# Transformer layers on one core: w2 loaded in blocks of six, and the task scheduler's cost model and priorities replaced

## The chip, the cores and the metric

The kernel runs on one core of a Trainium2 chip. The metric is the device time of one execution in microseconds (us), as the median of several executions. The changed kernel is timed in the same way. A difference counts as faster or slower when it exceeds 2%.

The engines are named as in the profile: PE is the matrix engine, PEld its weight loads, DVE the vector engine, ACT the activation engine, POOL the general-purpose engine, SP the engine that here does nothing but issue transfers (DMA).

## The reference

Two kinds of layer alternate on 2048 tokens of width 576, and the pair is run twice with the same weights. The core of it:

```python
def _A_ref(x, wqkv, wo):            # H = 32 heads of Dh = 18, window W = 256
    qkv = (x @ wqkv).reshape(B, S, 3, H, Dh) ...
    scores = jnp.einsum("bhqd,bhkd->bhqk", q, k) * (Dh ** -0.5)
    mask = (idx[:, None] - idx[None, :] >= 0) & (idx[:, None] - idx[None, :] < W)
    p = _softmax(jnp.where(mask, scores, -1e9), axis=-1)
    o = jnp.einsum("bhqk,bhkd->bhqd", p, v)
    return o.reshape(B, S, D) @ wo

def _B_ref(x, w1, b1, w2, b2):      # D = 576, F = 4608
    y = _layernorm(x)
    h = _gelu(jnp.einsum("bsd,df->bsf", y, w1) + b1)
    return jnp.einsum("bsf,fd->bsd", h, w2) + b2

x = x + _A_ref(_layernorm(x), A_wqkv, A_wo)
x = x + _B_ref(_layernorm(x), B_w1, B_b1, B_w2, B_b2)
x = x + _A_ref(...); x = x + _B_ref(...)      # the same once more
```

So there is sliding-window attention with many small heads, and a large MLP whose second norm is applied to a layer-normed input.

## The kernel before

The 16 token tiles of 128 rows are cut into chunks of four tiles. Two layer pairs make eight chunks, numbered 0 to 7. Each chunk passes through these parts, and the parts of neighbouring chunks overlap:

- **q**: the projections to q, k and v, five matmuls of 288 columns for each half (line 665), copied out of PSUM by DVE (lines 687, 700); q and k are then transposed by transfers issued on SP (line 707).
- **ea, eb**: attention for head groups 0 to 3 and 4 to 7. Scores are four row-tiled matmuls at a time (line 735), exp on ACT (744), window masks on POOL (765), then the products with v (782), all into the PSUM bank 7. DVE divides by the row sums (792, 797) into `attq`.
- **t**: the tail. `attq` is transposed to `attT` by a transfer on SP (826), multiplied by wo (665), added to the residual (816), normalised (603, 608) and transposed again (623).
- **ga, gb**: the first MLP matmul for each half of F (lines 863 and 875), gelu on ACT (878).
- **ma, mb**: the second MLP matmul with w2 for each half (903), added to the residual (816, or 819 for the last layer).

Nothing of this order is written down by hand. Every piece is a task with an engine, the names it reads and writes, an estimated cost and a priority. A list scheduler in Python runs when the kernel is built, keeps a clock for each engine, takes the task that can start first (ties by priority), and so fixes the order of instructions on each engine and which PSUM bank each accumulation uses. The chip executes these fixed orders, with semaphores for the dependencies. The estimated costs are used for nothing else.

```python
key = (round(st, 3), t.prio, t.idx)
...
if t.eng == "pe" and st < self.warm_until and st - free["pe"] > 0.4:
    self.keep_warm(free["pe"], st, bank_free, extra)     # adds idle-filling matmuls (line 567)
```

Until a modelled time of 140 us the scheduler fills gaps that it expects on PE with matmuls on a tile of zeros (`warm`). Their results are not used.

The part that handles a transfer in the model, and the load of w2, are the places where the change acts:

```python
            if t.dma is not None:
                if t.eng == "sp":
                    over = sum(q[2] for q in queued) + t.desc - self.ring
                    # ... cut: waits until the ring has room ...
                done = max(dma_free, st + t.cost + t.lat) + t.move
                ...
                dma_free = done if t.eng == "sp" else dma_free + t.move
```

```python
    def w2_load(hf, prio, gate=False):
        for pr in range(NFH // 2):                          # NFH = 18
            f0 = hf * NFH + 2 * pr
            dma("sp", w2_sb[:, 2 * pr:2 * pr + 2, :], B_w2[f0 * P:(f0 + 2) * P, :].rearrange("(w p) d -> p w d", p=P),
                reads=[f"h{2 * pr}"] if gate else [], writes=[f"w2s{pr}"], cls="w2", ring=9, cost=0.55, lat=2.0, move=0.88, desc=256, prio=prio)
```

The second MLP matmul reads w2 in groups of six of these row tiles:

```python
                for f0 in range(0, NFH, 6):
                    def fn(e, hh=hh, b=b, f0=f0, i=i):
                        for fl in range(f0, f0 + 6):
                            ins = e.matmul(bank(b)[:, 0:HB], hT[:, fl, i * 128:(i + 1) * 128], w2_sb[:, fl, hh * HB:(hh + 1) * HB],
                                           start=(fl == 0), stop=(fl == NFH - 1))
                    add("pe", fn, reads=[f"h{fl}" for fl in range(f0, f0 + 6)] + [f"w2s{fl // 2}" for fl in range(f0, f0 + 6)], writes=[b],
                        cost=6 * mm_cost(HB), prio=prio + 0.05 * i, alloc=((b,) if f0 == 0 else ()))
```

`PL.nudge` is a table of numbers added to the priorities of named parts of named chunks ("t0", "q4.3", "ma3"), found by a search over the model.

The softmax here doesn't subtract the row's maximum and nothing guards it: scores larger than these inputs give would overflow.

## Time and profile before

| what | value |
|---|---|
| time, median of 3 | 945.84 us (945.45 to 946.3) |
| span of the profiled execution | 940.9 us |
| PE busy | 910.2 us, 97% of the span, 9394 matmuls |
| ACT busy | 593.4 us, 63% |
| POOL busy | 372.1 us, 40% |
| DVE busy | 319.3 us, 34% |
| mean granted clock of PE | 0.996 |
| moved by DMA | 130.10 MB, mean 138 GB/s |

The profile page gives busy time for each engine, then the span in 40 slices, the DMA queues, the chain of work that ended last, the costliest groups of instructions, and the transfers. [...] 2304 matmuls of mean 287 ns are busy for only 318.0 us. How closely matmuls follow one another is read from the distance between their starts. The list of waits says for how long an engine stood idle and what ended that.

### The profile page before, as it was taken

The page shows a single profiled execution, that of the slowest core. Times are in us where ns is not written, and L with a number is a line of the kernel's source. Part 1 is how long each engine was busy: PE and PEld are TensorE (multiplying, and loading weights), DVE is VectorE, ACT ScalarE, POOL GpSimd, SP SyncE. Part 2 cuts the span into 40 slices and gives each one's busy share as a digit, 9 for nine tenths or more (in the row PEclk, how much of TensorE's full clock was granted, in tenths as well). Part 3 has the DMA queues.
Part 4 walks back from the last instruction along what each step waited for, and adds up shares of the span by engine and source line. Part 5 has one row for each costly group of instructions (what it writes and reads, how often), then busy time and mean ns, then how long its engine had stood idle before and what let it go on. Part 6 is the DMA issues. An engine that isn't in the chain of part 4 may idle for free. (4 is left out here: it accounts for less than half of the span.)

```text
span 940.9 us, 22724 instructions
## 1 busy us (share of the span) xinstructions
PE 910.2 (97%) x9394; PEld 559.5 (59%) x9394; DVE 319.3 (34%) x796; ACT 593.4 (63%) x717; POOL 372.1 (40%) x507
## 2 busy tenths in 40 slices
PE   9888998999999999989999999999999999999998
PEld 6555474664755747455674666656566574656556
DVE  6647132641217511154420832135132330241001
ACT  3787675576756658656465567756776587852541
POOL 3877352353514425144250644515443163720100
PEclk9999999999999999999999999999999999999999
DMA  9995729725196160965439434594526916094440
GB/s 225 153 219 113 212 60 247 191 56 169 21 218 163 16 204 13 249 130 140 133 45 270 79 93 123 99 252 77 158 71 121 252 52 203 13 233 140 151 140 26
DMA packets 232470, 130.10 MB, mean 138 GB/s; under 512 B 142384, under 2 KB 230192, under 8 KB 232368
## 3 DMA queue, kind: packets, MB, share of 16 engines
q1 hardware_dynamic: 223056, 120.96, 53.8%
q0 software_dynamic: 6880, 5.03, 3.7%
q10 hardware_dynamic: 2432, 2.65, 0.9%
q8 instruction: 75, 1.23, 0.5%
q14 instruction: 27, 0.22, 0.1%
HBM read 91.87 MB, written 2.36 MB: 100 GB/s over the span
## 5 line engine op out<-in xcount | busy, mean ns | idle before, releaser
L744 ACT ACTIVATE pT<-ps 128x1024 bf16<-128x1024 f32 (+2 forms) x384 | 348.3, 970 | 138.7 <-PE ps L735 137.6
L765 POOL TENSOR_SCALAR_AFFINE_SELECT pT<-pT 128x512 bf16<-128x512 bf16 (+1 forms) x368 | 281.8, 789 | 288.9 <-ACT pT L744 258.8
L903 PE MATMUL ps<-w_sb,hT 128*128 128x288 bf16 x2304 | 318.0, 287 | 3.1 <-DVE x_res L816 1.8
L878 ACT ACTIVATE hT<-ps,b1col 128x512 bf16<-128x512 f32 x288 | 197.0, 688 | 176.1 <-PE ps L875 175.9
L875 PE MATMUL ps<-xnTm,w_sb 128*128 128x512 bf16 x1152 | 263.8, 380 | 0.0
L903 PEld LDWEIGHTS ps<-w_sb,hT 128*128 128x128 bf16 x2304 | 212.0, 98 | 74.8 <-issue 15.1
L875 PEld LDWEIGHTS ps<-xnTm,w_sb 128*128 128x128 bf16 x1152 | 106.2, 98 | 142.0 <-issue 26.6
L816 DVE TENSOR_TENSOR x_res<-ps,x_res 128x288 f32<-128x288 f32 x160 | 71.2, 449 | 312.0 <-PE ps L903 242.9
L665 PE MATMUL ps<-wqkv,xnTa 128*128 128x288 bf16 x960 | 136.9, 288 | 6.3 <-DVE qn L700 4.1
L665 PEld LDWEIGHTS ps<-wqkv,xnTa 128*128 128x128 bf16 x960 | 86.4, 98 | 42.5 <-DVE qn L700 8.6
L782 PEld LDWEIGHTS ps<-vA,pT 128*128 128x128 bf16 x2880 | 94.8, 96 | 25.3 <-issue 9.7
L782 PE MATMUL ps<-vA,pT 128*128 128x20 bf16 x2880 | 100.4, 171 | 3.5 <-POOL pT L765 2.7
L700 DVE CAST qn<-ps 128x288 bf16<-128x288 f32 x120 | 54.3, 455 | 106.1 <-PE ps L665 103.5
L885 POOL TENSOR_TENSOR x_res<-x_res,b2bc 128x576 f32<-128x576 f32 x32 | 44.9, 1402 | 97.1 <-ACT hT L878 97.1
L735 PE MATMUL ps<-qT,kT 32*128 32x384 bf16 (+2 forms) x1216 | 64.4, 277 | 3.4 <-DMA kT<-qn 1.2
L591 POOL TENSOR_SCALAR vtmp<-mv_all 128x1 f32<-128x1 f32 (+1 forms) x43 | 8.8, 205 | 116.9 <-DVE mv_all L582 115.7
L665 PE MATMUL ps<-wo_sb,attT 128*128 128x288 bf16 x320 | 45.5, 289 | 6.7 <-DMA attT<-attq 5.8
L580 DVE BATCH_NORM_STATS2 st_all<-x_res 128x6 f32<-128x288 f32 x104 | 44.8, 447 | 7.5 <-DMA x_res<-in_A_x_dram 6.3
L863 PE MATMUL ps<-xnTm,w_sb 64*128 64x512 bf16 x288 | 45.3, 384 | 1.0 <-ACT pT L744 0.7
L603 DVE TENSOR_SCALAR xn<-x_res,mv_all,rstd 128x576 bf16<-128x576 f32 x52 | 38.9, 754 | 15.2 <-DMA xnTm<-xn 5.8
L665 PEld LDWEIGHTS ps<-wo_sb,attT 128*128 128x128 bf16 x320 | 29.6, 98 | 19.9 <-DMA attT<-attq 6.7
L819 DVE TENSOR_TENSOR xn<-ps,x_res 128x288 bf16<-128x288 f32 x32 | 14.4, 454 | 77.2 <-PE ps L903 75.6
(39 smaller groups left out, 270.3 us busy)
## 6 DMA issues: line engine op xcount, KB each, us to landing
w_sb<-in_B_w_dram SPq DMA_DIRECT2D x144, 288.0 KB, 4.5
w_sb<-in_B_w_dram SPq DMA_DIRECT2D x72, 512.0 KB, 4.5
w_sb<-in_B_w_dram SPq DMA_DIRECT2D x144, 32.0 KB, 4.1
x_res<-in_A_x_dram POOLq DMA_DIRECT2D x4, 1152.0 KB, 7.8
out_dram<-xn SPq DMA_DIRECT2D x16, 144.0 KB, 1.8
wqkv<-in_A_wqkv_dram ACTq DMA_DIRECT2D x3, 576.0 KB, 7.2
hT<-in_A_x_dram SPq DMA_DIRECT2D x2, 576.0 KB, 4.4
wo_sb<-in_A_wo_dram ACTq DMA_DIRECT2D x1, 576.0 KB, 6.6
```

What stands on the lines that cost most here:

```text
L665: ins = e.matmul(bank(bs[o])[:, 0:HB], lhs(c), rhs(c, o * HB), start=(c == 0), stop=(c == KD - 1))
L700: add("dve", lambda e, b=bs[o], dst=dst: e.tensor_copy(dst, bank(b)[:, 0:HB].rearrange("p (h d) -> p h d", d=DH)), reads=[bs[o]], writes=[ ...
L735: ins = e.matmul(two(bs[j // 2])[:, j % 2, col:col + nq * 128], k_of(T0 + so)[0][32 * j:32 * j + 32, g, :], qs[32 * j:32 * j + 32, g, qo * ...
L744: add("act", lambda e, h2=h2: e.activation(pT[:, sl, 2 * h2:2 * h2 + 2, lo:hi], two(bs[h2])[:, :, lo:hi], ACT.Exp, scale=SCALE), reads=[bs ...
L765: add("pool", lambda e, ap=ap, pat=pat, sgn=sgn, kind=kind: e.affine_select(ap, ap, pattern=pat, compare_op=(ALU.is_ge if kind == "d" else ...
L782: ins = e.matmul(bank(B_O)[:, o:o + VW], pT[:, sl, j, col + qi * 128:col + (qi + 1) * 128], vA[:, (T0 + so) % VS, 4 * g + j, :], start=(fi ...
L816: add("dve", lambda e: e.tensor_tensor(x_res[:, t, sl], bank(b)[:, 0:HB], x_res[:, t, sl], ALU.add), reads=[b], writes=[f"x{t}h{hh}"], cos ...
L863: ins = e.matmul(bank(bk)[:, 0:n], w1_sb[64 * b:64 * b + 64, sl, col:col + 128], xnTm[64 * b:64 * b + 64, k % 2, 4, 0:n], start=True, stop ...
L875: ins = e.matmul(bank(bk)[:, 0:n], w1_sb[:, sl, col:col + 128], xnTm[:, k % 2, c, 0:n], start=False, stop=(c == 3))
L878: add("act", lambda e, ff=ff, fl=fl, bk=bk: e.activation(hT[:, fl, 0:n], bank(bk)[:, 0:n], ACT.Gelu_apprx_tanh, bias=b1col[:, ff:ff + 1]), ...
L885: add("pool", lambda e, t=t: e.tensor_tensor(x_res[:, t, :], x_res[:, t, :], b2bc[:, :], ALU.add), reads=["b2", f"h{fs[0]}"], writes=X(t), ...
L903: ins = e.matmul(bank(b)[:, 0:HB], hT[:, fl, i * 128:(i + 1) * 128], w2_sb[:, fl, hh * HB:(hh + 1) * HB], start=(fl == 0), stop=(fl == NFH ...
```

## The change

The change has two parts. It computes the same thing.

**w2 in blocks of six.** Each half of w2 (18 row tiles of 128 x 576) is loaded by three transfers of six tiles instead of nine of two, so that one transfer brings just what one group of six matmuls reads.

**The scheduler's model and priorities.** The costs of the tasks are replaced by values taken from traces aligned with the tasks one by one. A latency between an engine's end and the next engine's start is given separately (`lat`). The model of the transfers keeps one queue for each issuing engine, lets queues that are busy at once slow each other down, and limits the ring for each. The table of priorities was searched anew, under random delays of the transfers. None of these numbers exists on the chip. They act only through the order of tasks, the choice of PSUM banks and the number of idle-filling matmuls.

```diff
-        for pr in range(NFH // 2):
-            f0 = hf * NFH + 2 * pr
-            dma("sp", w2_sb[:, 2 * pr:2 * pr + 2, :], ..., reads=[f"h{2 * pr}"] if gate else [], writes=[f"w2s{pr}"],
-                cls="w2", ring=9, cost=0.55, lat=2.0, move=0.88, desc=256, prio=prio)
+        for b in range(NFH // WB):                          # WB = 6
+            f0 = hf * NFH + WB * b
+            dma("sp", w2_sb[:, WB * b:WB * b + WB, :], ..., reads=[f"h{WB * b}"] if gate else [], writes=[f"w2s{b}"],
+                cls="w2", ring=NFH // WB, cost=0.55, lat=2.0, move=0.44 * WB, desc=128 * WB, prio=prio)
...
-reads=[...] + [f"w2s{fl // 2}" for fl in range(f0, f0 + 6)]
+reads=[...] + [f"w2s{f0 // WB}"]
...
-                done = max(dma_free, st + t.cost + t.lat) + t.move
-                if t.eng == "sp":
-                    queued.append((done - t.move, done, t.desc))
-                dma_free = done if t.eng == "sp" else dma_free + t.move
+                at = max(served.get(t.eng, 0.0), st + t.cost + min(t.lat, 2.0))
+                done = at + t.move
+                for o in served:
+                    if o != t.eng and served[o] > at:
+                        both = min(t.move, served[o] - at)
+                        served[o] += both
+                        done += both
+                served[t.eng] = done
+                q.append((done - t.move, done, t.desc))
+                done += max(0.0, t.lat - 2.0)
... (costs; some of them)
-  bn_stats cost=0.43            +  cost=0.37, lat=0.14
-  xd (64 columns) cost=0.12     +  cost=0.38, lat=0.14
-  copies of q, k, v cost=0.42   +  cost=0.375, lat=0.14
-  exp cost=0.12 + 2*n*0.00083   +  cost=0.07 + 2*n*0.00083, lat=0.17
-  gelu cost=0.2 + n*0.00087     +  cost=0.145 + n*0.00087, lat=0.17
-  residual cost=0.46            +  cost=0.375, lat=0.14
... (priorities; the first of some 50 each)
-    PL.nudge = {"ld0+": 36.49, "eb0": 11.82, "q1.0": -3.43, ..., "t0": -24.79, "ea1": -30.85, ...}
+    PL.nudge = {"le0+": 14.98, "q1.0": -6.62, "q1.1": 0.41, ..., "t0": 4.51, "ga0": -13.62, ...}
```

(The `...` inside a line, and the lines that start with it, mark cuts; the costs are condensed.)

## The prediction

> **What bounds the kernel now.** I read the page's busy shares first, then the matmul groups by shape, then the list of PE's waits, then the timeline around the two longest waits. The page's first part and slices (columns: busy us, share, instructions; then tenths per slice):

> ```profile
> PE 910.2 (97%) x9394; PEld 559.5 (59%) x9394; DVE 319.3 (34%) x796; ACT 593.4 (63%) x717; POOL 372.1 (40%) x507
> PE   9888998999999999989999999999999999999998
> PEclk9999999999999999999999999999999999999999
> ```

> PE is the bound from end to end, at full clock. No other engine passes 63%, so only two things can shorten this kernel: fewer or closer-packed matmuls, and fewer PE waits. The chain that ended last says the same (PE 19% of the span, everything else about 0%, though it reaches back only to 755 us).

> "97% busy" hides slack, since matmuls overlap. I took the start-to-start distance of every pair of neighbouring matmuls in the trace: 122 ns for 288 columns behind 288, 216 ns for 512, 25 ns for the 20-column products, about 220 ns for a 288-column one ahead of a row-tiled score (about 95 ns of changeover). Taking for each pair of kinds the lower quartile of these distances (the mean inside row-tiled packs), the old order adds up to 893.1 us. PE's matmuls run from 1.1 us to 937.6 us, that is 936.5 us. So 936.5 - 893.1 = **43.4 us are lost** to waits and slow stretches, and 3.3 us follow the last matmul (one addition, one output transfer). The largest visible losses (columns: us in total, times, longest us):

> ```profile
> PE ps L665 <- DMA attT<-attq: 5.8, 2, 3.1
> PE ps L665 <- DVE qn L700: 4.1, 9, 0.9
> PE ps L782 <- POOL pT L765: 2.7, 8, 0.6
> PE ps L735 <- DMA kT<-qn: 2.1, 2, 1.2
> PE ps L903 <- DVE x_res L816: 1.8, 4, 1.1
> PE ps L735 <- ACT pT L744: 1.6, 6, 0.4
> PE ps L903 <- DVE xn L819: 1.3, 1, 1.3
> ```

> The idle gaps of PE add up to 27.4 us, 11.4 of them in the first 100 us. There is one large item, the attT transposes: twice PE came to the wo product too early. The SP queue and PE around the second (start us, us, engine, line, operation):

> ```profile
> 402.22 1.68 SPq L707 DMA_TRANSPOSE kT<-qn  x1
> 404.00 1.73 SPq L524 DMA_DIRECT2D w_sb<-in_B_w_dram  x3
> 405.84 6.01 SPq L826 DMA_TRANSPOSE attT<-attq  x4
> ...
> 410.11 0.79 PE L665 MATMUL ps<-wo_sb,attT 128*128 128x288 bf16 x5 [2.68 <-DMA attT<-attq]
> ```

> `attq` was ready at 402.33 us, but a k transpose and three weight loads stood ahead in SP's fixed order; the transpose issued 3.5 us later and PE ran dry at 407.4.

> [...] The trace has 4.5 us for 288 KB, and 4.5 for 512 KB[...].

> **The change part by part.**

> *w2 blocks.* 144 issues become 48. At a median 0.515 us each (the weight issues in SP's queue) SP saves 96 x 0.515 = 49 us of issuing. SP only issues, and PE never waited visibly for w2, so it is worth nothing directly. The bytes are unchanged. The matmuls already read in sixes, so a slot comes free no later than before. [...] I compared the order of both programs, counting PE work (by the distances above) between the matmul that releases a w2 slot and the first matmul that reads the new content. The shortest was 7.8 us and is 7.1 us, in chunk 0's ma, where the load waits for the gelu; every other is over 10 us. There a wait of some 0.8 us is possible.

> *Same matmuls, other order.* The instruction counts of PE, ACT, DVE and POOL are equal, but for the zeros: 62 become 50. The old trace has them at 107 to 205 ns. Summing the new order with the same distances gives 890.3 us. **Gain 893.1 - 890.3 = 2.8 us** (2.6 of it zero matmuls; the changeovers to scores are equal within 0.2).

> *attT.* PE work between a chunk's last product with v and the first wo product, chunks 0 to 7, was 3.5, 6.6, 22.5, 4.8, 15.2, 6.2, 14.5, 6.7 us and is 6.9, 21.1, 7.0, 10.4, 12.6, 25.6, 10.8, 7.6. The two waits above belong to chunks 1 and 3 (6.6 and 4.8). A free queue needs about 5.1 us: 1.0 us for the division (in chunk 1 the last product with v ends at 152.09 us, the division at 153.09) and 4.0 us median to landing; in chunk 0, whose 3.5 us other waits stretched to 5.1 (68.6 to 73.69 us), PE did not wait for attT. The new minimum is 6.9. Directly ahead of the new chunk 3 transpose stands a q transpose instead of loads. I count **5.6 of the 5.8 us as gained**.

> *PSUM banks that DVE must empty.* DVE needs about 0.7 us. Old places with no PE work at all between use and reuse by the projections: 3 (two in chunk 7, 0.55 us idle each); new: 1, in the first chunk. **Gain 1.4 us**, with refill.

> *q and k transposes.* Old shortest distances 2.6 and 3.8 us, both waited (0.9 and 1.2). New: 4.9 and 5.0. **Gain 1.0 us**, but one of the new ones is at the start of chunk 7 (q at 5.6 and 6.1): **loss 0.8**.

> *The 1.3 us wait on L819* (DVE held by an xn slot still being transposed): half gained, 0.7.

> *New short distances.* Behind gb of chunk 0 a w2 group follows its gelu's matmul by 0.33 us (gelu takes 0.69) and a score reuses a bank written just before: 1.0 us. The bank of the v products is reused after 0.6 to 1.0 us four times where the division needs 1.0: 0.8 us. w2 above: 0.8 us. **Loss 2.6 us.**

> Sum: -2.8 - 5.6 - 1.4 - 1.0 - 0.7 + 0.8 + 2.6 = -8.1 us, all on PE and so on the path. 945.84 - 8.1 = **937.7 us**.

> **The rivals.**

> *A: the losses only move.* A new order has new near-misses, and distances do not show queueing behind ACT or the transfers. For it: 20 of the 27.4 us idle were many waits under 1.3 us that no one planned. Against: the new costs lie closer to the trace (the 64-column norm takes 0.468 us; the model had 0.12 and now 0.38 + 0.14). Then the gain is the 2.8 us alone: 943.

> *B: the blocks delay transposes.* 864 KB ahead of k, q or att transposes makes them late, and PE waits more for DMA. In the new order a block stands between the attT transposes of chunks 3, 4 and 5. For it: both old attT waits came from loads ahead. Against: the work to hide them is 10 us and more there. Two waits of 3 us: about 944; four: 950.

> *C: the better model removes most avoidable waits.* Of the 43.4 us lost, some 11 us in the first 100 us come from dependencies with little else to do, and about 12 us are not at task starts at all. That leaves about 20 us. Removing two thirds of it and the 2.8 us: 930.

> **Range and chances.** 937.7 lies between A and C. B and C are tails. I take 931 to 946. For over 2% the time must fall under 926.9, 18.9 us less, nearly all of the avoidable part: 0.05. Over 964.8 needs a systematic new wait, which the distances do not show: 0.02. The rest, 0.93, is within 2%.

> **What would show it.** In the changed profile: PE's wait for attT near 0 (step attT); 50 zero matmuls and the group about 2 us less busy; w2 transfers x48 at 864 KB landing in 5 to 7 us, without a PE wait for them over 1 us; idle gaps of PE near 20 us; start-to-start of 122 and 216 ns unchanged. Wrong would be: PE waits on DMA over 6 us (B), or idle about 27 us with other names (A), or under 14 us (C). Another granted clock would make it wrong for a reason outside all of this.

## The result, and the profile after

The changed kernel takes **938.13 us** (937.28 to 941.76) against 945.68 us for the kernel before, timed beside it: a ratio of 0.9926, with a 95% interval of 0.990 to 0.9953. Two further jobs with the unchanged pair gave 941.54 against 946.38 us (0.9947, 0.993 to 0.9965) and 940.42 against 944.68 us (0.9948, 0.993 to 0.9965). So the gain is 0.5 to 0.7%, which is 7.6, 4.8 and 4.3 us between the medians and "same" at the 2% line. The prediction was 937.7 us, a gain of 8.1 us.

The first part and two slice rows of the page after (busy us, share, instructions; then tenths per slice), and its first transfer:

```profile
PE 903.7 (96%) x9340; PEld 560.0 (60%) x9382; DVE 317.6 (34%) x796; ACT 593.8 (63%) x717; POOL 372.8 (40%) x507
...
PE   8888999999998999999999999999999999999998
...
PEclk9999999999999999999999999999999999999999
...
w_sb<-in_B_w_dram SPq DMA_DIRECT2D x48, 864.0 KB, 6.2
```

The program has 9382 matmuls, as PEld shows. 42 matmul records are missing from this profile, so the lower busy time of PE is no gain. The span of this execution is 939.8 us against 940.9 before, only 1.1 us less. It was the slowest of its four executions, and the profiled one of before (942.8 us) was faster than all its timed ones. A third profile of the changed kernel has all its records and a span of 936.5 us. The twelve largest of PE's waits in that one (us, times, longest us; xnTa and xnTm are the transposed normalised inputs of attention and of the MLP, w_sb holds the weights of the MLP, pT the exp of the scores):

```profile
PE ps L745 <- ACT pT L754: 3.5, 12, 0.5
PE ps L675 <- DVE qn L710: 3.2, 7, 0.9
PE ps L913 <- DMA w_sb<-in_B_w_dram: 2.3, 2, 1.3
PE ps L675 <- DMA xnTa<-xn: 2.1, 1, 2.1
PE ps L675 <- DVE x_res L826: 1.7, 2, 1.1
PE ps L873 <- DMA xnTm<-xn: 1.4, 1, 1.4
PE ps L745 <- issue: 1.2, 1, 1.2
PE ps L792 <- DVE attq L807: 1.1, 2, 0.8
PE ps L576 <- DVE warm L571: 1.1, 1, 1.1
PE ps L745 <- DMA kT<-qn: 1.0, 1, 1.0
PE ps L745 <- DVE xn L829: 1.0, 1, 1.0
PE ps L675 <- DMA attT<-attq: 0.9, 1, 0.9
```

The wait for attT fell from 5.8 us to 0.9 here (2.7 and 1.2 in the two other profiles). But 2.1, 1.4 and 2.3 us for xnTa, xnTm and w_sb stand where before there were 0.4 us for xnTa and none for the others. PE's idle gaps add up to 27.3 us in this profile and 27.4 in the first one of before. **The waits changed their names, and their sum did not fall.** (The other profiles of both kernels lack 42 records each, which lengthens the gaps: 31.2 us before, 32.7 and 32.5 us after.) That made the near-hit suspicious, and the experiments ask where the time really came from.

### The profile page after: what moved, and what is told of

The parts are those of the page before. It is cut to its first block, busy times and chain, and to the rows that moved or that the text cites. A ratio compares the mean times of both kernels' runs of the same rounds, so it can differ in the third digit from the quotient of the medians.

```text
span 939.8 us, 22499 instructions
## 1 busy us (share of the span) xinstructions
PE 903.7 (96%) x9340; PEld 560.0 (60%) x9382; DVE 317.6 (34%) x796; ACT 593.8 (63%) x717; POOL 372.8 (40%) x507
## 5 line engine op out<-in xcount | busy, mean ns | idle before, releaser
L912 PE MATMUL ps<-w_sb,hT 128*128 128x288 bf16 x2304 | 314.8, 286 | 2.0 <-DMA w_sb<-in_B_w_dram 1.0
L884 PE MATMUL ps<-xnTm,w_sb 128*128 128x512 bf16 x1110 | 259.3, 381 | 3.8 <-issue 1.9
L674 PE MATMUL ps<-wqkv,xnTa 128*128 128x288 bf16 x960 | 134.8, 288 | 7.4 <-DVE qn L709 3.6
L744 PE MATMUL ps<-qT,kT 32*128 32x384 bf16 (+2 forms) x1216 | 64.2, 277 | 6.0 <-ACT pT L753 2.1
L801 DVE RECIPROCAL rinv<-ps 128x16 f32<-128x16 f32 x64 | 16.3, 255 | 115.3 <-PE ps L791 114.8
L696 DVE CAST vA<-ps 128x288 bf16<-128x288 f32 x64 | 28.9, 455 | 76.3 <-PE ps L674 76.2
L611 DVE TENSOR_SCALAR xn<-x_res,mv_all,rstd 128x576 bf16<-128x576 f32 x52 | 36.1, 694 | 21.1 <-DMA xnTm<-xn 16.1
```

Of the source, the lines that this page charges most:

```text
L674: ins = e.matmul(bank(bs[o])[:, 0:HB], lhs(c), rhs(c, o * HB), start=(c == 0), stop=(c == KD - 1))
L744: ins = e.matmul(two(bs[j // 2])[:, j % 2, col:col + nq * 128], k_of(T0 + so)[0][32 * j:32 * j + 32, g, :], qs[32 * j:32 * j + 32, g, qo * ...
L884: ins = e.matmul(bank(bk)[:, 0:n], w1_sb[:, sl, col:col + 128], xnTm[:, k % 2, c, 0:n], start=False, stop=(c == 3))
```

## The experiments

Each was timed in five rounds beside the kernel before; a job is a set of versions timed together on one chip. Line numbers differ between runs, since each edit shifts the lines. "Clock" is the mean granted clock of PE over all timed executions. "Lost" is (1 - clock) x 940 us, the full-speed time that the throttle took away. The kernel before had 946.38 us and clock 0.9947 in job 1, 947.32 and 0.9942 in job 2, 944.68 and 0.9952 in job 3.

| run (job) | us | ratio | 95% interval | clock | lost, us |
|---|---|---|---|---|---|
| before again (1) | 946.82 | 1.0008 | 0.9992 to 1.0024 | 0.9945 | 5.2 |
| changed again (1) | 941.54 | 0.9947 | 0.9930 to 0.9965 | 0.9968 | 3.0 |
| old order, w2 in sixes (1) | 948.49 | 1.0018 | 1.0003 to 1.0033 | 0.9940 | 5.6 |
| new order, w2 in pairs (1) | 939.84 | 0.9933 | 0.9905 to 0.9960 | 0.9973 | 2.5 |
| before without mid zeros (2) | 949.88 | 1.0026 | 1.0009 to 1.0043 | 0.9924 | 7.1 |
| changed without mid zeros (2) | 936.67 | 0.9903 | 0.9879 to 0.9928 | 0.9968 | 3.0 |
| before, attT first (2) | 943.25 | 0.9966 | 0.9951 to 0.9981 | 0.9969 | 2.9 |
| new model, old priorities (2) | 958.47 | 1.0138 | 1.0103 to 1.0173 | 0.9933 | 6.3 |
| before, waits filled with zeros (3) | 940.96 | 0.9958 | 0.9942 to 0.9973 | 0.9989 | 1.0 |
| changed, third time (3) | 940.42 | 0.9948 | 0.9930 to 0.9965 | 0.9966 | 3.2 |
| pairs, no mid zeros (3) | 937.52 | 0.9911 | 0.9889 to 0.9933 | 0.9972 | 2.6 |
| the same, last attT first (3) | 937.51 | 0.9917 | 0.9897 to 0.9937 | 0.9970 | 2.8 |

### Both kernels again

No edit. Expected of the changed kernel and of the kernel before:

> The changed kernel itself, timed in five rounds, with a second profile. Its first profile has a span of 939.8 us, 4 us above two of its other executions, with a new wait of 2.7 us for an attT transpose and the clock down in two slices. Theory 1 (the gain is the new order of instructions): 0.992 of the time before, and a profile whose PE waits for attT, xnTa and xnTm are smaller than in the first profile when its span is nearer to 936 us. Rival (the gain is luck of the executions): 0.996 or more.

> The kernel before itself, with a second profile. Its first profile was an execution of 942.8 us, 3 us below its median. All theories: a ratio of 1.000 within the interval, which shows the noise. Theory 1: the waits of PE that vary between its two profiles are those for transfers (attT, kT, xnTa), by some 3 us in sum, and the waits for DVE and ACT repeat within 1 us.

The gain held at 0.53%, less than theory 1 expected but clear of the rival, and the kernel before repeated itself at 1.0008. In the changed kernel's second profile the wait for attT is smaller than in the first, as theory 1 had it (1.2 us), but the one for xnTa is larger (2.7 us, 2.1 in the first). Before's second profile has an attT wait of 5.9 us, so that wait is systematic and does not vary by 3 us as I had expected. The changed kernel's does vary: 2.7, 1.2 and 0.9 us in three profiles. The clock differs between the kernels: 5.0 us lost before (job 1), 3.0 after.

### Order or blocks?

Old order with blocks of six, in the loop that writes out the old kernel's instructions:

```diff
+            if t.dma == "w2":
+                pr = int(t.writes[0][3:])
+                if pr % 3:
+                    continue                 # loaded with the first of its three
+                t.fn = self.six[t.idx]       # one transfer of six row tiles
+                t.writes = tuple(f"w2s{pr + j}" for j in range(3))
```

> The order of before on PE, ACT, DVE and POOL, with w2 in three blocks of six a half: on SP each block stands where the first of its three pairs stood. Theory 1 (the order gains, the blocks don't): 0.999 to 1.001 of the time before. Rival 2 (the blocks gain, by fewer issues on SP, so that transposes behind them issue earlier): 0.993 to 0.996, and PE's wait for attT falls under 3 us. Rival 3 (the blocks cost, by delaying the transposes behind them): 1.002 or more.

New order with pairs, in the same loop of the changed kernel (the tasks that read w2 then wait for all three transfers):

```diff
+            if t.dma == "w2":
+                for j in range(3):           # three transfers of two row tiles
+                    self.S.add(t.eng, self.pairs[t.idx][j], t.reads, [f"{t.writes[0]}_{j}"], dma="w2", ring=9)
+                continue
```

> The order of the changed kernel on all engines, but each block of w2 is loaded by three transfers of two tiles, one behind the other, in the place of the one. Theory 1: 0.991 to 0.993 of the time before, as the changed kernel. Rival 2 (the blocks gain): 0.996 or more. Rival 3 (the blocks cost): under 0.990.

The order carries the whole gain: with pairs it is 0.9933, and with sixes it is 0.9947. "Order" here takes in the PSUM banks and the 12 zero matmuls fewer, which the scheduler decides with it. The blocks gain nothing. In the old order they cost 0.18% (rival 3, though small). What they delay is seen in PE's waits of that run; its longest attT wait is 5.6 us, where before had 3.1:

```profile
PE ps L675 <- DMA attT<-attq: 7.5, 4, 5.6
```

In the new order the blocks cost nothing that these intervals can separate.

### Costs or priorities?

```diff
-    PL.nudge = {"le0+": 14.98, "q1.0": -6.62, ...      # in the changed kernel: the new table out,
+    PL.nudge = {"ld0+": 36.49, "eb0": 11.82, ...       # the old one in
```

> The changed kernel (blocks of six, new costs and transfer model) with the old table of priorities. If the new costs alone bring the gain: 0.992 to 0.996 of the time before. If the gain comes from priorities searched for this model: 1.000 or more, since the old table was searched for another model; PE idle above 30 us.

1.0138: the new costs with priorities searched for the old ones are 13 us slower than before, and PE's idle gaps add up to 40.7 us instead of 27.4. The three largest waits:

```profile
PE ps L790 <- POOL pT L773: 6.9, 12, 1.3
PE ps L743 <- ACT pT L752: 6.7, 16, 1.1
PE ps L673 <- DMA attT<-attq: 5.1, 2, 2.6
```

The first two are what it adds (2.7 and 1.6 us before); the one for attT was 5.8 us before and did not grow. The new costs gain nothing with the old table. The new table on the old model was not tried, nor whether a second search on the old model would have gained as much.

### The zero matmuls

```diff
         for st, t in order:
+            if t.idx == -1 and st > 12.0:
+                continue
```

> The kernel before with the 21 matmuls on zeros left out that stand behind the start-up (41 at the start stay); all else in the same order. If they lie on PE's path, as the prediction counted them, they are worth 21 x 0.11 = 2.3 us: 0.9975 of the time before. Rival (they fill gaps in which PE waits anyway): 0.9995 to 1.0005, with as much more idle time on PE in the first 100 us. Third (they keep the clock up): above 1.001, with a lower granted clock in the first 100 us.

> The changed kernel without the 10 zero matmuls behind its start-up. On the path: 1.1 us less than the changed kernel (0.9947 in the last job), so 0.9935. Filling gaps: 0.9947. Keeping the clock: above 0.996.

In the old order 21 zero matmuls fewer (2.3 us) gained nothing; the kernel became 0.26% slower. In its profile PE's idle gaps add up to 33.7 us instead of 27.4, so the zeros lie in gaps. It also lost 7.1 us to the clock instead of 5.5 in that job, but not where the third expectation had it: the granted clock of the first 100 us is 0.98 with and without them, and the half-clock stretches that the profile adds are at 166.7, 409 and 651 us (granted clock 0.91 from 160 to 200 us, 0.98 from 400 to 480 and from 640 to 720), long after the last of these zeros (74.8 us). How leaving them out leads to those is not shown.

In the new order the kernel without 10 of them came to 0.9903, a larger gain than any of the three expectations allowed. That is below the intervals of the changed kernel in jobs 1 and 3, though inside that of the first result (0.990 to 0.9953), and it comes from another job. Pairs without zeros beside the changed kernel (job 3, below) point the same way, with intervals that still just overlap.

### The attT waits of the old order

The four attT transposes in the tails of chunks 1 and 3 are put ahead of the weight loads that stood before and between them on SP; nothing else changes.

```diff
-  chunk 3 on SP:  k4, w1 load (3 transfers), aT0, aT1, aT2, aT3, ...
+  chunk 3 on SP:  k4, aT0, aT1, aT2, aT3, w1 load (3 transfers), ...
-  chunk 1 on SP:  w2s2, w1 load (3), aT0, w1 and w2 loads, aT1, w1 and w2 loads, aT2, aT3, ...
+  chunk 1 on SP:  aT0, aT1, aT2, aT3, w2s2, w1 load (3), w1 and w2 loads, ...
```

> The kernel before with one thing moved on SP: in the tails of chunks 1 and 3 the four attT transposes stand ahead of the three or four weight loads that stood before or between them; order on PE, ACT, DVE and POOL unchanged. Theory (the two attT waits cost the time, 5.8 us of idle and the half-clock windows that follow waits of 3 us): PE's wait for attT under 2 us, clock 0.998, 0.992 to 0.995 of the time before. Rival (the wait is given back in the next wait, for the loads that were moved behind or for DVE): wait for attT under 2 us, but 0.998 or more, and waits for w_sb or xnTm in its place.

0.9966, a little short of the expected range: about 3.2 us. PE's wait for attT fell by 2.3 us (5.8 to 3.5), but at 186.74 us a wait for DVE appeared, which was 0.3 us before:

```profile
PE ps L746 <- DVE vA L698: 2.3, 2, 2.0
```

PE's idle gaps add up to 28.6 us, 27.4 before. So in this profile the idle time was given back, as the rival had it, and the clock, with 2.6 us less lost over all executions, makes up most of the gain. The wait of chunk 3 nearly went (2.7 to 0.8). That of chunk 1 fell from 3.1 to 2.2 only: the transposes now issue at 153.08 us, right behind the division, and the first still lands at 161.02. There the issue was not the cause. From 150 to 160 us of this run the DMA engines move 229 to 234 GB/s; among the transfers are two x_res loads of 1152 KB, issued by POOL at 145.27 and 148.32 us and landed at 151.22 and 160.57. Whether those loads held the transposes up was not shown: taking them away was not tried.

### What a wait costs beyond itself

The windows of the kernel before around its first attT wait (stretch; busy us and instructions of PE, PEld, DVE, ACT, POOL; then granted clock, DMA share, GB/s):

```profile
155.00:160.00 5.00, 3.88 (x20) 1.49 (x16) 0.64 (x2) 2.75 (x4) 0.00 (x0) 1.00 1.29 364
160.00:164.00 4.00, 2.04 (x12) 1.39 (x13) 3.06 (x12) 0.00 (x0) 0.00 (x0) 0.82 1.14 282
164.00:168.00 4.00, 4.00 (x19) 1.60 (x18) 2.30 (x7) 0.69 (x1) 1.94 (x4) 0.75 1.13 343
```

PE stood idle for 3.08 us up to 161.96. Then, working again, it ran below full clock: (1 - 0.82) x 4 + (1 - 0.75) x 4 = 1.7 us are lost, which is 3.4 us at half clock (162.60 to 166.01 us, granted 0.50). The test fills the two waits with useless work without shortening them:

```diff
+        for k in (1, 3):
+            i = next(... the first task on PE that reads aT0 in stage t1, t3)
+            z = Task(eng="pe", fn=lambda e, b=b: self.warm_fn(e, b, 20), writes=t.writes, ...)   # the bank about to be overwritten
+            order.insert(i, (st, z))
```

> The kernel before with 20 zero matmuls (20 x 0.107 = 2.1 us) on PE right ahead of the two wo products that wait 3.1 and 2.7 us for attT, in chunks 1 and 3, into the bank that the product is about to overwrite. They shorten no wait. If the half-clock windows after such waits cost time of their own: mean granted clock of the executions from 0.9945 to 0.997 or more, and 0.996 to 0.998 of the time before. If only the wait itself costs: 1.000, or up to 1.001 where the transposes land before the zeros are through.

0.9958, just beyond the good end of the expected range: **40 extra matmuls on zeros make the old kernel about 4 us faster**, and the clock goes from 0.9952 to 0.9989, which is 3.5 us less lost. Its windows at the same place:

```profile
160.00:164.00 4.00, 2.94 (x27) 2.31 (x25) 3.01 (x11) 0.51 (x1) 0.00 (x0) 1.00 1.14 308
164.00:168.00 4.00, 4.00 (x25) 1.89 (x23) 2.32 (x8) 1.12 (x2) 1.89 (x4) 1.00 1.12 354
```

The wait is still there (the products start at 163.02 us, 161.96 before), but the clock stays at 1.00, and in 164 to 168 us PE runs 25 matmuls instead of 19. The next wo products start at 168.23 us instead of 168.78, though the first ones started 1.06 us later. The same six matmuls in the timelines of before and of this run (start us, us):

```profile
163.75 1.65 PE L903 MATMUL ps<-w_sb,hT 128*128 128x288 bf16 x6
```

```profile
164.26 0.90 PE L910 MATMUL ps<-w_sb,hT 128*128 128x288 bf16 x6
```

### The combined versions

> The changed kernel again, beside its variants on the same chip: 0.9926 to 0.9947 of the time before, as in the two earlier jobs; mean granted clock about 0.997.

> The order of the changed kernel with w2 in pairs and without the 10 zero matmuls behind the start-up. Without zeros alone came to 0.9903, pairs alone to 0.9933, in different jobs. If both are effects of their own: 0.988 to 0.990, and 0.3 to 0.5% below the changed kernel of this job. If the differences were between jobs: the same as the changed kernel of this job within 0.2%.

> As pairs_no_zeros, and on SP the last attT transpose of chunk 2 stands ahead of the three weight loads that stood before it. If the wait for it (2.7, 1.0 and 1.3 us in the profiles) is on the path: 1 to 2 us below pairs_no_zeros and no wait for attT over 0.5 us. Rival (it is given back at once, since the next normalisation waits for DVE): within 0.5 us of pairs_no_zeros.

Pairs without mid zeros take 0.9911, 2.9 us less than the changed kernel in the same job, within the expected gap, though the level is a little above what was expected. They are clearly faster than the kernel before, and probably than the changed one (0.9889 to 0.9933 against 0.9930 to 0.9965). So is the changed kernel without zeros (0.9903); the two are not told apart.

The last version moved the one attT transpose that still waited (the fourth of chunk 2) ahead of three w1 loads. It gained nothing, and the waits of PE between 265 and 300 us say why; without and with the move:

```profile
PE ps L685 <- DMA attT<-attq: 2.6, 1, 2.6
```

```profile
PE ps L932 <- DMA w_sb<-in_B_w_dram: 1.8, 1, 1.8
```

The wait for attT is gone, and a wait for the weights that were moved behind takes its place: the result that the rival expected, though the wait is for loads and not for DVE.

## Why the prediction was right, and where it was right by luck

- **The bound, right.** PE stayed the bound, and its inner streams did not change (122 ns from start to start for 288 columns and 216 ns for 512, before and after).
- **w2 blocks worth nothing directly, right.** The landing time was 6.2 us, within the 5 to 7 expected. That was my estimate, like the 0.8 us wait in chunk 0's ma: the profile before has no load of 864 KB. The wait was 1.0, 1.3 and 1.0 us in three profiles. Two of them have a second wait for w2, which was not foreseen, of 0.8 and 1.3 us near 292 us. The cost that I gave to rival B appeared where the order was not searched for it (1.0018).
- **The 2.8 us of shorter order: the amount fits, the reason is not shown.** 2.6 of it were zero matmuls counted as work on the path. The two profiles with all records, the first before and the third after, differ by 4.4 us; 0.1 of it is idle time and 1.7 one half-clock stretch fewer (3.41 us at 0.50), which leaves 2.6. But leaving out 21 zeros in the old order turned into idle time, and in the new order leaving some out seems to gain; the sign depends on the order. The sum of distances cannot tell a filler in a gap from work.
- **attT 5.6 us, partly right.** The waits of chunks 1 and 3 went, as their distances said. But I counted only each chunk's first transpose. The fourth of chunk 2 stood behind three loads. In the first profile after, around 285 us:

```profile
281.41 1.73 SPq L532 DMA_DIRECT2D w_sb<-in_B_w_dram  x3
...
283.18 1.29 SPq L835 DMA_TRANSPOSE attT<-attq  x1
...
288.08 0.79 PE L674 MATMUL ps<-wo_sb,attT 128*128 128x288 bf16 x5 [2.69 <-DMA attT<-attq]
```

  The gain was 3.1, 4.6 and 4.9 us in the three profiles. (The 1.0 and 4.0 us of a free queue add up to 5.0, not 5.1; that changes nothing.)
- **PSUM banks 1.4 us, about right.** The waits of the projections on the copies of q and k fell from 4.1 to 3.6, 3.5 and 3.2 us, and those on the copies of v from 0.7 to 0.2: 1.0 to 1.4 us in all.
- **q and k, right.** kT fell from 2.1 to 1.0 us. The 0.8 us loss at the start of chunk 7 is there as "issue", 0.8 in the first profile and 1.2 in the third: the q transpose landed at 738.69 us and the scores began at 738.89.
- **L819 half gained, right:** 1.3 us became 0.7 in the first profile (1.0 in the third).
- **New short distances 2.6 us, too low.** gelu 0.9 (predicted 1.0), bank of the v products 2.5, 1.3 and 1.1 (0.8), w2 above. Not seen at all: xnTa 2.1 to 2.7 us near 51 us, where the transposes of that stretch take 5 to 8 us to land beside an x_res load (6.2 for xnTa in the first profile), and xnTm 1.3. The prediction has no term for them; the median landing of both is 2.6 us in the profile before. Waits for exp rose from 1.6 to 3.5 us.
- **What I left out: the clock.** "Full clock" was my reading of a row in tenths and of a mean of 0.996. The timed executions of before lose 5.0 us to half clock and those after 3.0 (job 1): 2.0 of the 4.8 us gained. The filled waits show that this is a cost of its own.

So of the 8.1 us, 5.3 were to come from idle time and did not; 2.8 from the shorter order fit what the two complete profiles leave; and the clock gave 2.0 us (job 1) and 1.4 us (job 3) that were not in the sum. Together these come near the 4.8 and 4.3 us measured there. That 937.7 us nearly equals the first result is luck as well: the four executions of the changed kernel there lost 1.9 us to the clock, those of the later jobs 3.0 and 3.2. Single profiles of one kernel differ by 3 us (939.8, 938.7 and 936.5 us after), so these shares are no finer than that.

Rival A (the losses only move) describes the idle time better than my sum did: its sign, idle about 27 us with other names, is what came. The sign of rival B, waits for DMA over 6 us, came too (8.0 us in the third profile), but it told nothing, since they were 8.3 us before.

## What to carry to other kernels

On an engine that is 97% busy, a wait of 2 to 3 us costs more than its length where the clock falls behind it: filling two such waits with useless matmuls brought about as much here (0.9958) as moving the transposes ahead did (0.9966). Not every such wait brings the clock down; the last section shows which did here. When an order is compared by distances, check every reader, and judge a transfer by its landing time in its own stretch, not by its median over the run. After a change with many small parts, compare the sum of the waits before crediting any one that vanished.

## What the runs showed of the hardware

The half-clock stretch at 162.6 us in the kernel before lasts 3.41 us at a granted clock of 0.50. Matmuls of 288 columns start 240 ns apart in it, 122 ns at full clock. It follows a wait of 3.08 us, but shorter waits had the same outcome. In the profiles half-clock stretches began after waits of 2.1 us (xnTa, at 52.8 us in the third profile after; granted clock 0.60 from 53 to 57 us) and 2.7 us (attT, at 288.9 us in the first; 0.61 from 288 to 292). One begins at 26.1 us in the kernel before, with 1.7 us idle in the 3.4 us ahead of it and no single wait over 1.3. A wait of 2.7 us at 410 us in the kernel before brought none.

```profile
159.18:162.60 3.42, 0.64 (x6) 0.52 (x7) 2.87 (x10) 0.42 (x1) 0.00 (x0) 1.00 1.20 256
162.60:166.01 3.41, 3.41 (x17) 1.60 (x14) 2.71 (x8) 0.00 (x0) 0.47 (x3) 0.50 1.12 359
404.94:408.36 3.42, 2.48 (x35) 1.66 (x32) 0.92 (x2) 1.94 (x2) 1.58 (x3) 1.00 1.03 241
408.36:411.77 3.41, 1.66 (x15) 1.11 (x16) 0.81 (x2) 0.60 (x2) 0.95 (x2) 1.00 0.82 120
411.77:415.18 3.41, 3.41 (x50) 2.72 (x48) 3.23 (x10) 1.57 (x3) 1.38 (x3) 1.00 0.24 48
```

Most of the first wait, 2.77 of 3.08 us, lies in one cell, and the next cell runs at half clock. The second is divided between two cells, and none follows. I counted each matmul as 0.42 ns per column from its start (216 ns for 512 columns), what overlaps only once, and twice the time at half clock (240 ns for 288 columns there, 122 elsewhere). The cell at 159.18 us is then filled to 18%, those at 404.94 and 408.36 us to 56 and 42%. In these two profiles, ahead of the cell in which the last matmul ends, four cells at full clock are filled under 36% (35 and 18% before, 24 and 18% after), and all four are followed by half clock. Of the 539 filled to 41% or more none is. The cells do not start with the program: the stretch that begins at 162.60 us in the first profile before begins at about 163.3 us in the second, worked out from its windows (granted clock 0.92 from 160 to 164 us and 0.66 from 164 to 168). That the same wait brings a half-clock stretch in one execution and none in the next would follow, but was not shown. All of this is read from the profiles; no run was made to test it.
